# A fused attention-and-GLU backward kernel: fewer all-DVE rows, shorter row groups, paired half matmuls, TensorE transposes at the end of the heads, reordered W_q^T and W_o loads

## The chip, the cores and the metric

The kernel runs on one core of a Trainium2 chip. The time is that of one execution on the device, in microseconds (us); a lower one is better. Comparisons are between medians of several executions. A core has a matrix engine (PE, with its weight loads PEld), a vector engine (DVE), a scalar engine (ACT), a general engine (POOL) and a queue engine (SP) that issues transfers. Each runs its own instructions in order and waits for the others by semaphores.

## The reference

The forward function and its gradient by every weight, by x, and by the key and value caches (S = 2048 rows, D = 576, H = 32 heads of 128, F = 4608):

```python
xn = _layernorm(x)
q = (xn @ wq).reshape(B, Sq, H, Dh).transpose(0, 2, 1, 3)
scores = einsum("bhqd,bhkd->bhqk", q, k_cache) * (Dh ** -0.5)
p = softmax(scores)
s = einsum("bhqk,bhkd->bhqd", p, v_cache).transpose(0, 2, 1, 3).reshape(B, Sq, H * Dh) @ wo
h = sigmoid(xn @ w_gate) * (xn @ w_up)
g = silu(h @ w_down)
out = x + s * g
_out, _vjp = jax.vjp(f, x, k_cache, v_cache, wq, wo, w_gate, w_up, w_down)
return (_out, *_vjp(grad_out))
```

The argument B_x is not used. All arrays are bf16.

## The kernel before

The program is a sequence of stages on one core, each fully unrolled, with the rows in 16 tiles of 128 (NT = 16) and D in four tiles of 128 and a last one of 64 (DL = 4 is its number, KL = 64).

*Stage A* (lines 191 to 349) norms x, makes gate and up products and stores three [2048, 4608] arrays a, b, h. Its last contraction tile has only 64 rows, and gate and up share one weight tile there: `rest` (298 to 303) issues a pair of matmuls, one on partitions 0 to 63 and one on 64 to 127. *Stage A2* (351 to 413) makes h @ w_down, and dS for the projection, kept transposed in `dsT`; the normed x is kept transposed in `xnT`.

*The heads* (416 to 806) take most of the time. A head is laid out in 64 units of its own time scale, HEAD = 64. In the first 32 (the P half) every two units hold one row of P: `s_half` twice (2 matmuls of 512 columns into one of two PSUM buffers of `ps_big`, then a DVE pass with a running minimum), then `s_exp` on ACT. In the second 32 (the dS half) they hold one row of dS: `dp_half` twice. Its second half always goes through DVE in one pass (`scalar_tensor_tensor`, line 592); its first half goes through ACT (line 595) and a DVE product (`ds_mul`, 599), but for the rows in `STT2`, which DVE takes wholly. P and dS of two rows (a pair, 1 MB) are then transposed by one DMA on the SP queue (`trans_dma`, 603), into one of four buffers (`wpt`), and `row_mm` (620) multiplies the result with V or K, four rows (a group) at a time, spread over ROW_W units from unit XR + 8g on. The key and value gradients (`kv_mm`, 641 and 644) are spread over the time that is left by `level`, which fills each unit up to an even load. Transposes on PE and projections for this head and the next one (`prep_...`, `proj`) stand at positions given in tables (QT_AT to QN_AT), and use one PSUM bank, `ps_tr`.

All of it is collected as (position, function) by `at` and `anchor`, sorted, and issued in that order; PE, DVE and ACT keep it (`MAN`), the SP and POOL queues get an order of the compiler's own. At the end of the last head `load_wo` (457) loads W_o over `xnT` and `dsT`, five loads on SP from unit 50 on in program order.

*The projection stage* (808 to 884) multiplies each row tile's transposed attention output (`oT`, loaded by a transposing DMA from `on2_d`, five buffers, line 843) with W_o, makes the output and `doB`, the gradient on the GLU's side, and transposes that into `doBT` (`transpose_doB`). Its fifth tile holds 64 rows of doB in partitions 64 to 127 and zeros below. W_down^T is loaded likewise by `load_wdT` (857), in three thirds, the two others during the next stage. PE, DVE, ACT, SP and POOL keep the program's order here.

*Stage B1* (886 to 981) runs over 18 blocks of 256 columns of F. `make_dh` makes dh for 16 row tiles, five matmuls of 256 columns each (the fifth with the zero half), two row tiles in one PSUM buffer of two, then an ACT copy and two DVE products. `make_dwd` makes the gradient of w_down for 128 rows, twice per block. Then the gradients of w_up and w_gate follow (967, and in column halves 975). `turn` (152) is called throughout: it transposes a stored key or value gradient of one head by DMA and stores the one loaded by the call before; there are 46 of them.

*Stage C2* (985 to 1056) makes the gradients of W_o and W_q, with W_up^T and W_gate^T loaded by the way. *The tail stage* (1058 to 1139) makes dx in eight blocks of 256 rows, each in eight passes (`do_pass`): three with du, three with dg, two with dq, the last two with W_q^T in four groups of eight heads (`load_wqT`). The first two blocks run their first six passes first and then the last two. `finish` ends a block. SP keeps the program's order in B1, C2 and the tail stage.

Of the kernel before, what the change touches and what calls it, by code (L numbers as in the profile page):

```python
# [13 lines left out]
P = 128  # L14
# [81 lines left out]
def kernel(  # L96
# [324 lines left out]
    STT2 = {0, 5, 10}  # L421
    with tc.tile_pool(name="ld2", bufs=2) as ld2, tc.tile_pool(name="ld1q", bufs=1) as ld1q, \
# [192 lines left out]

        def row_mm(bx, hs, T, rhs, qt, kt, sink):
# [81 lines left out]
        XR, ROW_W = 16.8, 6.9  # L698
# [3 lines left out]
        KT_AT, DON_AT, VT_AT, QN_AT = (37.2, 40.0, "s"), (8.6, 22.0, "v"), (0.2, 10.4, "s"), (24.2, 28.2, "s")  # L702
# [51 lines left out]
        WO_AT = 50.0  # L754
        MAN = {mybir.EngineType.PE, mybir.EngineType.DVE, mybir.EngineType.Activation}
        for h in range(H):
# [19 lines left out]
            for qt in range(NT):  # L776
# [32 lines left out]
    if True:  # L809
# [3 lines left out]
        nc.vector.memset(doBT[:P - KL, DL, :], 0.0)  # L813

        def transpose_doB(pool, st_):
# [5 lines left out]
            alt.copy(doBT[P - KL:, DL, cols], pt[P - KL:, DL, :])  # L821

# [6 lines left out]
        with tc.tile_pool(name="c1b", bufs=1, side="right", reuse_waits="tile") as blk, \  # L829
# [60 lines left out]
        with tc.tile_pool(name="b1o", bufs=2, reuse_waits="tile") as outp, tc.tile_pool(name="b1k", bufs=2, reuse_waits="tile") as tkp, tc.tile_pool(name="b1t", bufs=3, reuse_waits="tile") as tmpp, \  # L890
                tc.tile_pool(name="b1r", bufs=2, reuse_waits="tile") as dblk, \
                tc.tile_pool(name="b1l", bufs=1, reuse_waits="tile") as ldp, \
                tc.tile_pool(name="b1ps", bufs=2, space=PSUM, reuse_waits="tile") as ps, \
                tc.tile_pool(name="b1pa", bufs=2, space=PSUM, reuse_waits="tile") as psa, \
# [17 lines left out]
            for fb in range(F // FB):  # L912
# [5 lines left out]
                def make_dh():  # L918
                    for st in range(NT):
                        srows = slice(st * P, (st + 1) * P)  # L920
                        if st % 2 == 0:
                            dh = ps.tile([P, 2, FB], f32, name="dh")
                        for i, (d0, kd) in enumerate(dts):
                            kk = kfull(i, kd)
# [247 lines left out]
```

## Time and profile before

| what | us |
|---|---|
| median of 3 runs | 5063.81 (5054.67 to 5084.64) |
| the profiled execution | 5069.4 |
| its span, first to last instruction | 5067.4 |
| PE busy | 4914.0 (97%) |
| DVE busy | 3098.3 (61%) |
| ACT busy | 2390.4 (47%) |
| POOL busy | 1504.2 (30%) |
| heads without the last one | about 530 to 3530, 98.1 each from the tenth on |
| last head | 3530 to 3660 |
| projection stage | 3660 to 3804 |
| stage B1, 18 blocks | 3804 to 4391, 32.5 each |
| stage C2 | 4391 to 4643 |
| tail stage | 4643 to 5067 |

A line of the list of waits reads: engine, what it was about to do, what ended the wait, then total us, number, longest. In a timeline each row has start, length, engine, line, operation, output and inputs, shape and count, and in brackets the idle time before it and what ended it. "DMA to landing" is from a transfer's issue to its last byte. Busy time of PE counts pipelined matmuls, whose lengths overlap; their spacing is that of their starts.

### The profile page before, as it was taken

The page shows a single profiled execution, that of the slowest core. Times are in us where ns is not written, and L with a number is a line of the kernel's source. Part 1 is how long each engine was busy: PE and PEld are TensorE (multiplying, and loading weights), DVE is VectorE, ACT ScalarE, POOL GpSimd, SP SyncE. Part 2 cuts the span into 40 slices and gives each one's busy share as a digit, 9 for nine tenths or more (in the row PEclk, how much of TensorE's full clock was granted, in tenths as well). Part 3 has the DMA queues.
Part 4 walks back from the last instruction along what each step waited for, and adds up shares of the span by engine and source line. Part 5 has one row for each costly group of instructions (what it writes and reads, how often), then busy time and mean ns, then how long its engine had stood idle before and what let it go on. Part 6 is the DMA issues. An engine that isn't in the chain of part 4 may idle for free.

```text
span 5067.4 us, 107190 instructions
## 1 busy us (share of the span) xinstructions
PE 4914.0 (97%) x45178; PEld 3188.2 (63%) x45968; DVE 3098.3 (61%) x4853; ACT 2390.4 (47%) x3035; POOL 1504.2 (30%) x2197
## 2 busy tenths in 40 slices
PE   9998999999999999999999999999889999999999
PEld 3344777777766666666666666666547778755454
DVE  6555878887887888888788888888533222110101
ACT  5533656665666666566566666656302222100000
POOL 4322333333333333333333333332322323211000
PEclk9999999999999999999999999999999999999999
DMA  7875999999999999999999999999999988899996
GB/s 255 271 219 140 204 201 207 202 209 208 209 205 208 209 201 207 208 203 207 209 209 212 205 208 210 204 202 213 222 182 273 232 225 218 253 267 235 199 211 140
DMA packets 2865204, 1077.14 MB, mean 213 GB/s; under 512 B 2672336, under 2 KB 2795216, under 8 KB 2864720
## 3 DMA queue, kind: packets, MB, share of 16 engines
q1 hardware_dynamic: 2779456, 784.45, 86.6%
q0 software_dynamic: 85264, 285.79, 19.7%
q8 instruction: 359, 5.88, 0.5%
q14 instruction: 125, 1.02, 0.1%
HBM read 172.54 MB, written 225.12 MB: 78 GB/s over the span
## 4 chain that ended last, share of the span: by engine, by line
PE 84%; DVE 5%; issue 4%; DMA 3%; POOL 3%; SPq 0%; ACT 0%; DVEq 0%; POOLq 0%; ACTq 0%
PE acc L620 16%; PE acckv L644 9%; PE acc L1101 7%; PE sp L556 7%; PE dp L589 6%; PE accw L967 5%; PE acckv L641 5%; PE accp L513 4%; PE dh L925 3%; PE acc L392 3%; PE accd L943 3%; PE g_ps L295 2%; PE acc L1025 2%; PE u_ps L295 2%; PE acct L520 2%
## 5 line engine op out<-in xcount | busy, mean ns | idle before, releaser
L568 ACT ACTIVATE Pq<-sneg,nm 128x2048 bf16<-128x2048 bf16 x512 | 1025.9, 2004 | 212.0 <-DVE sneg L558 169.3
L592 DVE SCALAR_TENSOR_TENSOR dSq<-dp,delta,Pq 128x1024 bf16<-128x1024 f32 x608 | 770.8, 1281 | 390.8 <-PE dp L589 384.4
L620 PE MATMUL acc<-Kn,dST 128*128 128x128 bf16 x8192 | 955.2, 219 | 22.5 <-DMA dST<-dSq 6.4
L620 PE MATMUL acc<-Vn,PT 128*128 128x128 bf16 x8192 | 957.9, 219 | 15.9 <-DMA PT<-Pq 6.5
L620 PEld LDWEIGHTS <-dST 128*128 128x128 bf16 x8192 | 670.9, 98 | 363.9 <-DMA dST<-dSq 10.7
L620 PEld LDWEIGHTS <-PT 128*128 128x128 bf16 x8192 | 665.3, 98 | 329.8 <-DMA PT<-Pq 7.6
L558 DVE TENSOR_SCALAR_CACHE_REDUCE sneg<-sp,nm 128x1024 bf16<-128x1024 f32 x512 | 656.7, 1283 | 132.8 <-PE sp L556 101.1
L595 ACT ACTIVATE t<-dp,negdelta 128x1024 bf16<-128x1024 f32 x416 | 463.5, 1114 | 510.3 <-PE dp L589 419.8
L558 DVE TENSOR_SCALAR_CACHE_REDUCE sneg<-sp 128x1024 bf16<-128x1024 f32 x512 | 624.7, 1220 | 92.9 <-PE sp L556 45.7
L589 PE MATMUL dp<-VT,dOT 128*128 128x512 bf16 x1943 | 587.1, 379 | 26.4 <-DVE dSq L592 26.2
L556 PE MATMUL sp<-KT,QT 128*128 128x512 bf16 x1922 | 583.2, 380 | 7.3 <-DVE sneg L558 6.5
L644 PE MATMUL acckv<-Pq,dOn 128*128 128x512 bf16 x1312 | 487.5, 380 | 5.8 <-POOL dOn L576 5.8
L644 PE MATMUL acckv<-dSq,Qn 128*128 128x512 bf16 x1355 | 490.2, 380 | 1.2
L599 DVE TENSOR_TENSOR dSq<-t,Pq 128x1024 bf16<-128x1024 bf16 x416 | 304.5, 732 | 0.0
L576 POOL TENSOR_TENSOR dOn<-dOn,rinv_all 128x256 bf16<-128x256 bf16 x256 | 157.2, 614 | 390.2 <-DVE rinv_all L572 322.7
L967 PEld LDWEIGHTS <-xn_all 128*128 128x128 bf16 x2304 | 224.2, 98 | 27.8
L1117 DVE SCALAR_TENSOR_TENSOR junk<-dxn,xn_all 128x576 f32<-128x576 f32 x16 | 12.1, 758 | 370.9 <-ACT dxn L1112 370.9
L1101 PEld LDWEIGHTS <-cf 128*128 128x128 bf16 x2304 | 145.8, 98 | 145.6 <-DMA cf<-du_d 5.6
L513 PE MATMUL accp<-xnT,wq_h 128*128 128x512 bf16 x609 | 227.8, 384 | 4.4 <-ACT KT L40 1.1
L641 PE MATMUL acckv<-dOn,Pq 128*128 128x128 bf16 x2304 | 217.3, 219 | 2.8 <-POOL dOn L576 1.4
L674 POOL TENSOR_TENSOR prod<-ou,dOn 128x512 f32<-128x512 bf16 x128 | 154.8, 1209 | 207.5 <-ACT ou L40 206.7
L641 PE MATMUL acckv<-Qn,dSq 128*128 128x128 bf16 x2304 | 213.9, 219 | 1.4
(188 smaller groups left out, 7461.6 us busy)
## 6 DMA issues: line engine op xcount, KB each, us to landing
out_dram<-turn SPq DMA_DIRECT2D x46, 512.0 KB, 4.7
h_d<-h_row POOLq DMA_DIRECT2D x48, 384.0 KB, 2.9
a_d<-a_row POOLq DMA_DIRECT2D x48, 384.0 KB, 3.4
b_d<-b_row POOLq DMA_DIRECT2D x48, 384.0 KB, 4.5
a_blk<-a_d SPq DMA_DIRECT2D x18, 1024.0 KB, 6.0
b_blk<-b_d SPq DMA_DIRECT2D x18, 1024.0 KB, 21.7
du_d<-du_blk POOLq DMA_DIRECT2D x18, 1024.0 KB, 8.7
dg_d<-dg_blk POOLq DMA_DIRECT2D x18, 1024.0 KB, 11.7
```

The lines of the kernel that those rows point to most:

```text
L513: nc.tensor.matmul(acc[:], lhsT=w[:, i, :], rhs=(srcT if i < DL else xnT)[:, i, cs], start=(i == 0), stop=(i == DL))
L556: nc.tensor.matmul(sp[:, c * CH:(c + 1) * CH], lhsT=hs.QT[:, qs], rhs=hs.KT[:, hf * HW_ + c * CH: hf * HW_ + (c + 1) * CH], start=True, st ...
L558: nc.vector.tensor_scalar(sneg[:, hf * HW_:(hf + 1) * HW_], sp[:], -SCALE, None if hf == 0 else nm[:, hf - 1:hf], op0=ALU.mult, op1=ALU.mi ...
L568: nc.scalar.activation(Pq, sneg[:], AF.Exp, bias=nm[:, hf:hf + 1], scale=-1.0, accum_out=hs.rs_all[:, qt:qt + 1])
L589: nc.tensor.matmul(dp[:, c * CH:(c + 1) * CH], lhsT=hs.dOT[:, qs], rhs=hs.VT[:, hf * HW_ + c * CH: hf * HW_ + (c + 1) * CH], start=True, s ...
L592: nc.vector.scalar_tensor_tensor(dSq[:, hsl], dp[:], hs.delta[:, qt:qt + 1], Pq[:, hsl], op0=ALU.subtract, op1=ALU.mult)
L595: nc.scalar.activation(t[:], dp[:], AF.Identity, bias=hs.negdelta[:, qt:qt + 1], scale=1.0)
L620: nc.tensor.matmul(bx.acc[:, j, :], lhsT=T[qt][:, kt, :], rhs=getattr(hs, rhs)[:, kt, :], start=(kt == 0), stop=(kt == NT - 1))
L641: nc.tensor.matmul(bx.acc[i][:, j * P:(j + 1) * P], lhsT=slabs[qt][:, k0 + j * P:k0 + (j + 1) * P], rhs=w, start=(qt == 0 and j == 0), sto ...
L644: nc.tensor.matmul(bx.acc[i][:], lhsT=w, rhs=slabs[qt][:, k0:k0 + CH], start=(qt == 0), stop=(qt == NT - 1))
L967: nc.tensor.matmul(acc[:kd, :FB], lhsT=xn_all[:, st, d0:d0 + kd], rhs=blk_[:, st, :], start=(st == 0), stop=(st == NT - 1))
L1101: nc.tensor.matmul(accs[sl][j][:, :nn], lhsT=ch[:, kk, sl * P:(sl + 1) * P], rhs=w_[:, n0:n0 + nn], start=(pi == 0 and kk == 0), stop=(las ...
```

## The change

1. `STT2` goes from rows 0, 5 and 10 to row 0. `ROW_W` goes from 6.9 to 6.7 units, the first position of `DON_AT` from 8.6 to 8.9, and the last quad of the first kv group comes no earlier than 8.1 units after its base instead of 7.4.
2. `load_wo` issues from ACT instead of SP, in 15 pieces of two or three heads, one every 4 units from unit 1.3 of the last head on.
3. In the last head the P pair of rows 14 and 15 and the dS pairs of rows 6 and 7 and of rows 14 and 15 are transposed by PE (`pe_pair`) and copied from PSUM, and not by DMA.
4. `doBT`'s fifth tile gets the 64 rows in both partition halves, and so does the last tile of W_down^T, by a POOL transfer from partitions 64 to 127 to 0 to 63 that waits for the transposing one. `make_dh` is made in halves of eight row tiles, with four PSUM buffers: the first four matmuls of all eight tiles, then the eight fifth ones in pairs, one on each half of the partitions, of row tiles two apart. In all blocks but the first the order is now dh half, dwd half, dh half, dwd half. dwd has one PSUM pair in place of two.
5. Stage C2 has one `turn` less and the tail stage's turns stand in passes 1, 3 and 5 of blocks 2 to 6. W_q^T groups 2 and 3 are loaded two passes later in the second block. The last passes of the first two blocks alternate: pass 6 of both, then pass 7 of both.

```diff
-    STT2 = {0, 5, 10}
+    STT2 = {0}
-            nc.sync.dma_start(dst, A_wo[h0 * P:h1 * P, :].rearrange("(h p) d -> p h d", p=P))
+            nc.scalar.dma_start(dst, A_wo[h0 * P:h1 * P, :].rearrange("(h p) d -> p h d", p=P))
...
+        def pe_pair(T, pairs, qt, name, n, pool, tag, i, eng):
+            if i == 0:
+                t_ = wpt.tile([P, 2 * NT, P], bf, name=name, tag="PT")
+                for j in range(2):
+                    T[qt + j] = t_[:, j * NT:(j + 1) * NT, :]
+            pt = pool.tile([P, n, P], bf, name="ptr", tag=tag)
+            for m in range(n):
+                j, kt = divmod(i * n + m, NT)
+                nc.tensor.transpose(pt[:, m, :], pairs[qt][:, j, kt * P:(kt + 1) * P], ident[:])
+            j, kt = divmod(i * n, NT)
+            alt.copy(T[qt + j][:, kt:kt + n, :], pt[:], eng=eng)
...
-        XR, ROW_W = 16.8, 6.9
+        XR, ROW_W = 16.8, 6.7
-        KT_AT, DON_AT, VT_AT, QN_AT = (37.2, 40.0, "s"), (8.6, 22.0, "v"), (0.2, 10.4, "s"), (24.2, 28.2, "s")
+        KT_AT, DON_AT, VT_AT, QN_AT = (37.2, 40.0, "s"), (8.9, 22.0, "v"), (0.2, 10.4, "s"), (24.2, 28.2, "s")
-                    pos = max(pos, 4.0 * (n // 4) + 7.4, DON_AT[1] + 2.0 if n >= NT else 0.0)
+                    pos = max(pos, 4.0 * (n // 4) + (8.1 if n // 4 == NT // 2 - 1 else 7.4), DON_AT[1] + 2.0 if n >= NT else 0.0)
-        WO_AT = 50.0
+        WO_AT = [(i, min(i + 2, 14)) for i in range(0, 14, 2)] + [(14, WX)] + [(i, min(i + 2, WX + WD)) for i in range(WX, WX + WD, 2)]
+        P_PE = {NT - 2: (35.5, 37.5, 39.5, 41.5)}
+        DS_PE = {6: (48.5, 50.5, 52.5, 54.5), NT - 2: (65.5, 67.0)}
...
-                    at(p1 + PT_AT, trans_P, hs, qt - 1)
-                    at(p2 + DST_AT, trans_dS, hs, qt - 1)
+                    if h == H - 1 and qt - 1 in P_PE:
+                        for i, p_ in enumerate(P_PE[qt - 1]):
+                            at(b + p_, pe_pair, hs.PT, hs.Pp, qt - 1, "PT", 8, ps_tr, "tr", i, "s")
+                    else:
+                        at(p1 + PT_AT, trans_P, hs, qt - 1)
+                    if h == H - 1 and qt - 1 in DS_PE:
+                        for i, p_ in enumerate(DS_PE[qt - 1]):
+                            if len(DS_PE[qt - 1]) == 4:
+                                at(b + p_, pe_pair, hs.dST, hs.dSp, qt - 1, "dST", 8, ps_tr, "tr", i, "s")
+                            else:
+                                at(b + p_, pe_pair, hs.dST, hs.dSp, qt - 1, "dST", NT, ps_big, "big", i, "sv"[i])
+                    else:
+                        at(p2 + DST_AT, trans_dS, hs, qt - 1)
...
-        for k, (h0, h1) in enumerate(((0, 8), (8, 16), (16, WX), (WX, WX + 7), (WX + 7, WX + WD))):
-            if h0 < H - 1:
-                at(bl + WO_AT + 3 * k, load_wo, h0, min(h1, H - 1))
+        for k, (h0, h1) in enumerate(WO_AT):
+            at(bl + 1.3 + 4 * k, load_wo, h0, h1)
...
-        nc.vector.memset(doBT[:P - KL, DL, :], 0.0)
...
             alt.copy(doBT[P - KL:, DL, cols], pt[P - KL:, DL, :])
+            alt.copy(doBT[:KL, DL, cols], pt[P - KL:, DL, :])
...
                 nc.sync.dma_start_transpose(wdT_h[k][:, i, :], B_w_down[k * FH:(k + 1) * FH, dlo[i]:dlo[i] + P])
+                if i == DL:
+                    nc.gpsimd.dma_start(wdT_h[k][:KL, DL, :], wdT_h[k][P - KL:, DL, :])
...
-                tc.tile_pool(name="b1ps", bufs=2, space=PSUM, reuse_waits="tile") as ps, \
-                tc.tile_pool(name="b1pa", bufs=2, space=PSUM, reuse_waits="tile") as psa, \
+                tc.tile_pool(name="b1ps", bufs=4, space=PSUM, reuse_waits="tile") as ps, \
+                tc.tile_pool(name="b1pa", bufs=1, space=PSUM, reuse_waits="tile") as psa, \
...
+                def make_dh(half):
+                    w_ = wdT_h[fb * FB // FH]
+                    sts = range(half * NT // 2, (half + 1) * NT // 2)
+                    dhs = [ps.tile([P, 2, FB], f32, name="dh") for _ in sts[::2]]
+                    for k, st in enumerate(sts):
+                        for i in range(DL):
+                            nc.tensor.matmul(dhs[k // 2][:, k % 2, :], lhsT=doBT[:, i, st * P:(st + 1) * P], rhs=w_[:, i, fh],
+                                             start=(i == 0 and k % 2 == 0), stop=False)
+                    for k in (0, 1, 4, 5):
+                        for j in range(2):
+                            rs = slice(j * KL, (j + 1) * KL)
+                            st = sts[k + 2 * j]
+                            nc.tensor.matmul(dhs[k // 2 + j][:, k % 2, :], lhsT=doBT[rs, DL, st * P:(st + 1) * P], rhs=w_[rs, DL, fh],
+                                             start=False, stop=(k % 2 == 1))
+                    for k, dh in enumerate(dhs):
...
                 else:
-                    make_dh()
                     for fl in range(FB // P):
+                        make_dh(fl)
                         make_dwd(fl)
...
-                if hg < NHG - 1:
+                if hg < NHG - 2:
                     turn(tkp)
...
+            WQ_AT = [(0, 3), (0, 5), (1, 3), (1, 5)]
...
-                if sbi == 0 and pi in (3, 5):
-                    load_wqT((3, 5).index(pi))
-                elif sbi == 1 and pi in (1, 3):
-                    load_wqT(2 + (1, 3).index(pi))
-                elif sbi and sbi < NSB - 1 and (pi % 4 == 1 or (pi == 3 and sbi > 1)):
+                if (sbi, pi) in WQ_AT:
+                    load_wqT(WQ_AT.index((sbi, pi)))
+                elif 1 < sbi < NSB - 1 and pi in (1, 3, 5):
                     turn(tkp)
...
-            order_ = [(sbi, pi) for sbi in range(2) for pi in range(NPF)] + [(sbi, pi) for sbi in range(2) for pi in range(NPF, len(passes))]
+            order_ = [(sbi, pi) for sbi in range(2) for pi in range(NPF)] + [(sbi, pi) for pi in range(NPF, len(passes)) for sbi in range(2)]
```

More of the change, by code (lines that the diff above doesn't have):

```diff
@@ L1 @@
+import itertools
 from contextlib import ExitStack
@@ L917 @@
                 dg_blk = dblk.tile([P, NT, FB], bf, name="dg_blk")
[L918 to L924, printed above, removed]
-                            nc.tensor.matmul(dh[:, st % 2, :], lhsT=doBT[:kk, i, srows], rhs=wdT_h[fb * FB // FH][:kk, i, fh], start=(i == 0), stop=(i == DT - 1))
-                        if st % 2 == 1:
-                            s2 = slice(st - 1, st + 1)
-                            dhc = tmpp.tile([P, 2, FB], bf, name="dhc")
-                            nc.scalar.copy(dhc[:], dh[:])
-                            nc.vector.tensor_tensor(du_blk[:, s2, :], dhc[:], a_blk[:, s2, :], op=ALU.mult)
-                            nc.vector.tensor_tensor(dg_blk[:, s2, :], dhc[:], b_blk[:, s2, :], op=ALU.mult)
-                    nc.gpsimd.dma_start(du_d[:, fcols].rearrange("(t p) f -> p t f", p=P), du_blk[:])
-                    nc.gpsimd.dma_start(dg_d[:, fcols].rearrange("(t p) f -> p t f", p=P), dg_blk[:])
@@ L1079 @@
             accs_ = {}
+            ncq = itertools.count()
+            WQ_AT = [(0, 3), (0, 5), (1, 3), (1, 5)]
             def do_pass(sbi, pi):
```

13 lines of the change are left out of this document (11 added, 2 removed).

## The prediction

> **What bounds the kernel now.** First the page's head, then busy time by stage, to see which engine is full where.
>
> ```profile
> span 5067.4 us, 107190 instructions
> 530.00:3530.00 3000.00, 2933.32 (x29506) 2011.22 (x30058) 2424.89 (x3520) 1921.14 (x2153) 1022.14 (x1425) 1.00 1.17 207
> 3530.00:3660.00 130.00, 108.22 (x944) 69.20 (x961) 78.58 (x113) 57.16 (x64) 35.17 (x48) 0.93 1.14 219
> 3660.00:3804.00 144.00, 130.46 (x1073) 69.24 (x1093) 48.38 (x75) 7.69 (x31) 33.78 (x63) 0.96 1.16 191
> ```
>
> Columns: stretch, its length, busy time of PE, PE's weight loads, DVE, ACT and POOL, clock, DMA share, GB/s. PE is full in the heads (first row: all but the last head), and short by 22 us in the last head (second row) and by 14 us in the projection after it (third). So a gain comes either from fewer PE slots or from PE's stops. The list of PE's waits, over heads 0 to 30, the last head, the projection stage and the tail stage:
>
> ```profile
> PE dp L589 <- DVE dSq L592: 25.1, 30, 0.8
> PE acckv L644 <- POOL dOn L576: 5.1, 22, 1.4
> ...
> PE acc L872 <- DMA oT<-on_d: 7.4, 1, 7.4
> PE acc L620 <- DMA PT<-Pq: 6.1, 3, 4.5
> PE acc L620 <- DMA dST<-dSq: 3.6, 2, 2.9
> ...
> PE acc L872 <- DMA oT<-on_d: 12.3, 2, 9.8
> ...
> PE acc L1101 <- DMA cf<-du_d: 4.9, 2, 3.1
> PE acc L1101 <- DMA cf<-dg_d: 2.0, 1, 2.0
> ```
>
> One dp stop of 0.84 us falls in each head. The timeline of DVE and PE shows where:
>
> ```profile
> 2032.79 2.47 DVE L592 SCALAR_TENSOR_TENSOR dSq<-dp,delta,Pq 128x1024 bf16<-128x1024 f32 x2
> 2034.12 0.59 PE L589 MATMUL dp<-VT,dOT 128*128 128x512 bf16 x2 [0.85 <-DVE dSq L592]
> ```
>
> That is row 10, whose two halves both go to DVE, just behind a delta reduction, a kv copy and a product (three at 0.68). PE needs the first half's PSUM buffer and gets it 0.85 late. Rows 0 and 5 stop nobody.
>
> Next to PE runs the SP queue, the instructions of the transposing line:
>
> ```profile
> L603 SPq DMA_TRANSPOSE PT<-Pq  x256: 4778/5628/8863, 484.3 to 3590.6; - x128
> L603 SPq DMA_TRANSPOSE dST<-dSq x256: 4716/5892/9762, 530.8 to 3643.5; - x128
> ```
>
> Added up in the timeline these 16 per head hold SP 5.98 us each, with 0.1 between: 97.3 us of a head's 98.1. They start on average 3 to 4 us after their slab is complete, and land 4 us (median) before the first weight load that reads them. SP is thus nearly a second bound.
>
> **Row 0 alone on DVE; shorter row groups.** Row 10's first half becomes an ACT pass (1.11, mean of L595) plus a DVE product (0.68) in place of 1.28 of DVE. ACT stands idle for the 2.06 us up to 2031.55, and the copies of wo's transpose (0.86 for two) move behind the new pass. The buffer is free at about 2032.2 where PE wants it at 2033.3, so the stop goes: 25.1. Row 5 the same, for nothing. ACT gains 2.2 us per head at 64% busy (1921/3000). The last quad of the first kv group, put at 8.1 rather than 7.4, waits out POOL's scaling: 5.1 + 1.2 (the like wait of L641). Together 31 us, or 1.0 a head, for a pace of 97.1.
>
> But SP needs 97.3. Going through the 480-odd pairs with their own durations, against a PE that has these stops no longer, the pairs come late by 13 to 16 us in sum; with each transpose 1% shorter by 2, with 1% longer by 32. Row groups of 6.7 instead of 6.9 units free a buffer 0.3 us earlier and ask for a second pair 0.15 us earlier: nothing either way against 4 us. I take **-15**, bounds -31 and 0.
>
> **Last head.** Three pairs (P rows 14-15, dS rows 6-7 and 14-15) leave SP: 3 x 6 = 18 us of it. PE makes 96 transposes instead; eight of L520 take 0.49 us on their weight loads, so 12 x 0.49 = 5.9 us, and ACT eight-block copies of 0.99 each, with ACT at 44% (57/130) in that stretch, and one larger DVE copy. No projection for a next head uses that PSUM bank any more. Removed: the dST stops (3.6) and the stop on the first oT (7.4), as SP reaches oT earlier. The PT stops (6.1) came while 4.5 MB of W_o were issued between transposes from SP; the same bytes now go in 15 pieces from ACT over the whole head, so half the bytes remain beside the P transposes: 4 of the 6.1 go. After its two long stops PE ran at half speed for 5.5 and 4.6 us (512-column matmuls at 0.63 instead of 0.38): 5.0 lost, 4 regained. Fifteen issues of 0.58 (SP's row for these loads) hold ACT 9 us, which it has. Sum: -3.6 - 7.4 - 4 - 4 + 5.9 = **-13**; bounds -20 (all stops and clock go) and +6 (only the transposes are felt).
>
> The Trainium skill (DMA: Bandwidth & Descriptors, Issuing engines are not separate DMA queues) says that another issuing engine saves only issue time, since all share the same 16 DMA engines. By it only SP's 3.3 us of W_o issues (three of 0.58, 0.58 and 0.95) would come back of the PT stops, near the 4 taken.
>
> **Projection stage.** From its ninth tile on, each oT load is issued just as its buffer is freed (five buffers, unchanged), and 8 to 15 us per transpose beside the 144 KB loads and stores makes the 12.3 us late. An earlier start of the queue does not change that part: 0, bounds -14 and +8. New: POOL waits for the last W_down^T transpose before it copies its 64 rows, with the row loads for tiles 14 and 15 behind it. That transpose landed at 3796.5, when PE ended tile 14 (3795.6); loads land 4 us later: DVE's last products and two doB transposes may slip, **+1** (0 to 3). The two later copies stand before an h block that is needed over one block (32 us) later. Sixteen small doBT copies and one memset lie on DVE and ACT, idle there: 0.
>
> **dh pairs.** Of 40 slots per half block, 8 fifth matmuls become 4 pairs with 64 rows each. Stage A's timeline has such pairs:
>
> ```profile
> 149.70 0.81 PE L295 MATMUL u_ps<-wu_sb,xnT 128*128 128x512 bf16 x3
> 150.44 0.39 PE L303 MATMUL g_ps<-wl_sb,xnT 64*128 64x512 bf16 x1
> 150.44 0.39 PE L303 MATMUL u_ps<-wl_sb,xnT 64*128 64x512 bf16 x1
> 150.67 0.38 PE L303 MATMUL g_ps<-wl_sb,xnT 64*128 64x512 bf16 x1
> ...
> 150.98 1.04 PE L295 MATMUL g_ps<-wg_sb,xnT 128*128 128x512 bf16 x4
> ```
>
> and the chain of waits has a whole dh block (start, length):
>
> ```profile
> 3838.32 8.84 PE dh L925 x80
> ```
>
> The two start together, so a pair costs one slot; but going in costs 0.09 more than the 0.22 spacing (150.44 instead of 150.35), coming out again 0.09. A dh slot is (8.84 - 0.27) / 79 = 0.108. Per half: 4 x 0.108 saved less 0.18, 0.25; two weight loads per slot may cost another 0.01 each. 36 halves: **-8**, bounds -15.6 (no cost of switching) and +6.5 (pairs run one by one, 36 x 0.18). One accumulator pair instead of two is hidden: half a dh (4.1 us) lies between the halves of dwd, and its copies take 0.69. The last product of a half ends about 3.5 us after its dh, under a dwd half of 3.9.
>
> The Trainium skill (TensorEngine Tiling (Array Packing), Key Properties) says that changing the tiling mode drains the engine. A full drain, as an estimate 0.27 - 0.11 = 0.16 per switch, would leave 0.11 per half, 4 us in all; stage A's 0.09 is shorter, and the sum goes by it.
>
> **Tail.** One turn fewer ahead of the first cf load, W_q^T groups 2 and 3 two passes later, pass 6 of both column blocks before pass 7: the late cf loads get 6.6 us of transposes (five at 1.3) less ahead of them. The cq loads (5 us each, PE 7.7 a pass) follow just in time. **-5** of 6.9; bounds -7 and 0. The last turn is now loaded in the sixth block's sixth pass and stored by the call behind the loop, after the last dx store on SP: a turn store takes 3.2 us to land, the dx store 1.8, so **+2**.
>
> **Sum.** -15 - 13 + 0 + 1 - 8 - 5 + 2 = -38. The profiled execution's 5069.4 (span 5067.4 and 2.0 around) would be 5031; the median of the runs shown, 5063.8, is 5.6 lower, so **5026**.
>
> **Rivals.**
> *All stops go*: SP keeps up (its durations shrink with PE's stops), -31; last head -20; dh -10; tail -5. -66, 4998. For it: 52 places in heads 2 to 30 where SP stood idle, 46 us in sum. Against: nine heads in a row (14 to 22) without any.
> *SP takes the stop over*: heads give nothing, the last head -5, dh -8, tail -3: -16, 5048. For it: those nine heads averaged 98.4 us.
> *Pairs don't pair*: 256-column pairs need two weight loads in 0.108 us. dh +6.5 instead of -8: 5040. Against: L975, two column halves of the same width, one pair per 0.11.
> *ACT held by its loads* (slower): if each W_o issue holds ACT until the transpose before it has landed (9.2 us, median landing), eight of them in the P half cost 74, less some 6 us of slack there: 68 - 38 = +30, 5094. It decides from 5.5 us per issue on (44 - 6 = 38). Against: SP's own W_o issues took 0.58 to 0.95 directly behind transposes. None of the rows shows an issue from ACT during transposes.
>
> **How the numbers follow.** Forecast 0.60 (its own range 5012 to 5040), all stops go 0.16, SP takes over 0.15, no pairs 0.03, ACT held 0.06. A change under 0.5% (25 us: 5038.5) can't be told from none. Faster: 0.56 of the forecast's 0.60, all of 0.16, 0.02 of the third: 0.74. Slower: the last, 0.06. Same: 0.20. Range 4996 to 5052: from the first rival through the second.
>
> **What would show it.** dp's waits on DVE fall from 30 to about none, and waits on PT and dST rise from 3 to some 15 us over the heads: right; if they rise by 30, the second rival. dh blocks of 2 x 4.1 us with K=64 matmuls starting in twos: right; one by one, the third. No 7.4 us stop at the first oT. ACT's W_o issues under 1 us each. A turn store landing last. It is wrong if head pace stays at 98.1, or if a new stop appears in each head.

## The result and the profile after

| | before | after |
|---|---|---|
| median, us | 5066.76 (17 runs, 5048.19 to 5084.64) | 5039.6 (17 runs, 5021.89 to 5055.04) |
| ratio, 95% interval | | 0.995 (0.9935 to 0.9965) |
| profiled execution, its span | 5069.4, 5067.4 | 5044.53, 5042.7 |

The changed kernel is 27 us faster. The forecast was 38 (5026), its range 4996 to 5052. A table by stage shows how the parts of the sum came out. Its limits are starts of single instructions in the two profiled executions: first exp of head 0, first exp of head 31, last row matmul of the last head, last matmul with W_o, last of B1, last of C2, last matmul of PE, end.

| stage | before | after | difference | forecast |
|---|---|---|---|---|
| up to head 0's first exp | 479.7 | 486.4 | +6.7 | 0 |
| 31 heads | 3048.7 | 3042.8 | -5.9 | -15 |
| last head | 128.6 | 117.8 | -10.8 | -13 |
| projection stage | 146.7 | 135.3 | -11.4 | +1 |
| B1 | 587.3 | 581.4 | -5.9 | -8 |
| C2 | 251.8 | 253.8 | +2.0 | 0 |
| tail and end | 424.7 | 425.3 | +0.6 | -3 |
| span | 5067.4 | 5042.7 | -24.7 | -38 |

The first row's code is unchanged. All later profiles of this study have 478 to 483 there; this execution was long by chance.

The page's head, and the stages' busy times (stretch, length, busy PE, PE's weight loads, DVE, ACT, POOL, granted clock, DMA share, GB/s):

```profile
span 5042.7 us, 108373 instructions
PE 4952.7 (98%) x46064; PEld 3173.9 (63%) x46064; DVE 3049.5 (60%) x4861; ACT 2466.5 (49%) x3116; POOL 1532.1 (30%) x2200
```
```profile
530.00:3530.00 3000.00, 2967.92 (x30135) 2017.22 (x30133) 2393.28 (x3525) 1992.14 (x2221) 1052.24 (x1431) 1.00 1.18 207
3530.00:3648.00 118.00, 109.95 (x1057) 72.18 (x1056) 78.81 (x115) 69.41 (x75) 34.18 (x45) 0.99 1.16 217
3648.00:3783.00 135.00, 132.07 (x1109) 69.76 (x1107) 45.95 (x81) 13.33 (x38) 36.22 (x66) 1.00 1.15 198
```

In the last head PE was idle 22 us of 130 and is now idle 8 of 118; in the projection stage it was 14 of 144 and is 3 of 135. PE's waits over heads 0 to 30, the last head, the projection stage and the tail stage:

```profile
PE acc L633 <- DMA dST<-dSq: 16.6, 13, 2.8
PE acc L633 <- DVE dq_n L704: 12.3, 30, 0.4
PE dp L590 <- DVE dSq L593: 1.1, 2, 0.8
PE acc L633 <- DMA PT<-Pq: 0.8, 3, 0.3
PE acckv L657 <- POOL dOn L577: 0.3, 1, 0.3
...
PE acc L899 <- DMA oT<-on_d: 3.5, 1, 3.5
PE acc L633 <- DMA PT<-Pq: 2.3, 3, 1.1
...
PE acc L899 <- DMA oT<-on_d: 2.9, 3, 1.8
...
PE acc L1137 <- DMA cf<-du_d: 2.8, 1, 2.8
PE acc L1137 <- DMA cq<-dq_d: 2.6, 2, 2.3
```

The dp stop is gone (25.1 to 1.1), the stops on dOn too (6.5 to 0.3). Against this stand 12.3 us of new stops on `dq_n`, 0.41 in each head, which nothing in the forecast's sum names, and waits on dST that rose from 2.8 to 16.6. The timeline (start, length) shows the new stop:

```profile
2558.01 0.59 PE L557 MATMUL sp<-KT,QT 128*128 128x512 bf16 x2
2558.44 0.38 PE L657 MATMUL acckv<-dSq,Qn 128*128 128x512 bf16 x1
2559.23 0.22 PE L633 MATMUL acc<-Kn,dST 128*128 128x128 bf16 x1 [0.41 <-DVE dq_n L704]
2559.29 0.61 PE L521 MATMUL acct<-ident,dOT 128*128 128x128 bf16 x8
...
2557.28 1.28 DVE L559 TENSOR_SCALAR_CACHE_REDUCE sneg<-sp,nm 128x1024 bf16<-128x1024 f32 x1 [0.41 <-PE sp L557]
2558.49 0.69 DVE L704 TENSOR_TENSOR dq_n<-acc,rsc 128x512 bf16<-128x512 f32 x1
```

PE begins the fourth dS row group (unit 8.8 of the next head) and needs the PSUM buffer that DVE is still emptying for the third. The eight transposes of dOT, moved from 8.6 to 8.9, now come right behind that matmul; at 8.6 they lay in front of it.

Some late dST pairs make long stops. Behind the two longest (2.67 in head 7, 2.80 in head 23) stands a stretch at half clock. Head 23, POOL's timeline, then the stretches:

```profile
2813.62 0.60 POOL L481 DMA_DIRECT2D Vn<-in_A_v_cache_dram  x1 [4.21 <-PE acc L633]
2816.84 0.83 POOL L695 DMA_DIRECT2D on_d<-o_n  x1 [0.29 <-POOL o_n L694]
2820.66 0.54 POOL L494 DMA_DIRECT2D wo_h<-in_A_wo_dram  x1 [2.99 <-PE acct L502]
```
```profile
2819.00:2824.00 5.00, 5.00 (x54) 3.43 (x52) 4.59 (x6) 3.55 (x5) 1.72 (x4) 1.00 1.51 141
2824.00:2829.00 5.00, 2.24 (x15) 0.96 (x12) 2.48 (x3) 1.11 (x1) 0.98 (x2) 1.00 0.94 174
2829.00:2834.00 5.00, 4.96 (x31) 2.91 (x32) 1.88 (x2) 1.27 (x2) 0.00 (x0) 0.66 1.25 238
```

In the same 10 us as a V load, a row store and a W_o load, one transpose held SP for 9.9 us instead of 6 and landed 15.6 us after its issue, at 2829.0. PE stands for 2.8 us in the second row, and in the third its clock is 0.66.

### The profile page after: what moved, and what is told of

It reads as the page before. It is cut to its first block, busy times and chain, and to the rows that moved or that the text cites. A ratio compares the mean times of both kernels' runs of the same rounds, so it can differ in the third digit from the quotient of the medians.

```text
span 5042.7 us, 108373 instructions
## 1 busy us (share of the span) xinstructions
PE 4952.7 (98%) x46064; PEld 3173.9 (63%) x46064; DVE 3049.5 (60%) x4861; ACT 2466.5 (49%) x3116; POOL 1532.1 (30%) x2200
## 4 chain that ended last, share of the span: by engine, by line
PE 86%; DMA 7%; issue 3%; DVE 2%; POOL 1%; SPq 0%; ACT 0%; DVEq 0%; POOLq 0%; ACTq 0%
PE acc L633 16%; PE acckv L657 11%; PE sp L557 8%; PE acc L1137 8%; PE dp L590 7%; PE acckv L654 5%; PE accw L1002 5%; PE accp L514 5%; DMA dST<-dSq 3%; PE acc L393 3%; PE accd L977 3%; PE dh L951 2%; PE acc L1060 2%; PE acct L521 2%; PE acc L899 2%
## 5 line engine op out<-in xcount | busy, mean ns | idle before, releaser
L633 PE MATMUL acc<-Kn,dST 128*128 128x128 bf16 x8192 | 946.2, 219 | 30.8 <-DMA dST<-dSq 16.6
L593 DVE SCALAR_TENSOR_TENSOR dSq<-dp,delta,Pq 128x1024 bf16<-128x1024 f32 x544 | 694.7, 1282 | 394.3 <-PE dp L590 389.4
L633 PE MATMUL acc<-Vn,PT 128*128 128x128 bf16 x8192 | 920.3, 219 | 3.4 <-DMA PT<-Pq 3.1
L633 PEld LDWEIGHTS <-PT 128*128 128x128 bf16 x8192 | 653.8, 98 | 333.9 <-DMA PT<-Pq 6.1
L596 ACT ACTIVATE t<-dp,negdelta 128x1024 bf16<-128x1024 f32 x480 | 535.1, 1115 | 460.0 <-PE dp L590 455.8
L557 PE MATMUL sp<-KT,QT 128*128 128x512 bf16 x2048 | 610.8, 380 | 6.6 <-DVE sneg L559 6.5
L590 PE MATMUL dp<-VT,dOT 128*128 128x512 bf16 x2048 | 609.9, 379 | 2.1 <-DVE dSq L593 1.1
L657 PE MATMUL acckv<-dSq,Qn 128*128 128x512 bf16 x1472 | 537.5, 380 | 0.0
L657 PE MATMUL acckv<-Pq,dOn 128*128 128x512 bf16 x1472 | 528.8, 379 | 0.3 <-POOL dOn L577 0.3
L600 DVE TENSOR_TENSOR dSq<-t,Pq 128x1024 bf16<-128x1024 bf16 x480 | 343.0, 714 | 0.0
L1153 DVE SCALAR_TENSOR_TENSOR junk<-dxn,xn_all 128x576 f32<-128x576 f32 x16 | 12.1, 758 | 370.7 <-ACT dxn L1148 370.7
L1148 ACT ACTIVATE dxn<-acc 128x512 f32<-128x512 f32 (+1 forms) x32 | 12.9, 407 | 403.0 <-issue 301.6
```

The lines of the kernel that those rows point to most:

```text
L557: nc.tensor.matmul(sp[:, c * CH:(c + 1) * CH], lhsT=hs.QT[:, qs], rhs=hs.KT[:, hf * HW_ + c * CH: hf * HW_ + (c + 1) * CH], start=True, st ...
L590: nc.tensor.matmul(dp[:, c * CH:(c + 1) * CH], lhsT=hs.dOT[:, qs], rhs=hs.VT[:, hf * HW_ + c * CH: hf * HW_ + (c + 1) * CH], start=True, s ...
L593: nc.vector.scalar_tensor_tensor(dSq[:, hsl], dp[:], hs.delta[:, qt:qt + 1], Pq[:, hsl], op0=ALU.subtract, op1=ALU.mult)
L596: nc.scalar.activation(t[:], dp[:], AF.Identity, bias=hs.negdelta[:, qt:qt + 1], scale=1.0)
L633: nc.tensor.matmul(bx.acc[:, j, :], lhsT=T[qt][:, kt, :], rhs=getattr(hs, rhs)[:, kt, :], start=(kt == 0), stop=(kt == NT - 1))
L657: nc.tensor.matmul(bx.acc[i][:], lhsT=w, rhs=slabs[qt][:, k0:k0 + CH], start=(qt == 0), stop=(qt == NT - 1))
```

## The experiments

Each kernel is the changed one with the edit shown. The stage times below are from one profiled execution each, with the limits of the table above. As executions of one kernel differ by up to 48 us here, the stage that an edit touches tells more than the total.

| run | 31 heads | last head + projection | B1 | C2 | tail + end | median | ratio to before |
|---|---|---|---|---|---|---|---|
| before | 3048.7 | 275.3 | 587.3 | 251.8 | 424.7 | | |
| after | 3042.8 | 253.1 | 581.4 | 253.8 | 425.3 | 5039.6 | 0.995 (0.9935 to 0.9965) |
| e1_don | 3065.1 | 263.5 | 579.3 | 252.6 | 422.2 | 5030.4 | 0.9939 (0.9906 to 0.9972) |
| e2_skip | 3030.7 | 245.0 | 580.6 | 252.1 | 424.6 | 5015.9 | 0.9902 (0.9865 to 0.9939) |
| e3_heads | 3059.2 | 250.9 | 579.5 | 254.2 | 423.1 | 5047.0 | 0.9968 (0.9947 to 0.9989) |
| e4_lastdma | 3042.4 | 284.4 | 579.7 | 254.6 | 425.1 | 5057.9 | 0.9982 (0.9964 to 1.0) |
| e5_wosp | 3048.1 | 258.7 | 579.3 | 253.0 | 421.9 | 5037.2 | 0.9963 (0.9946 to 0.9979) |
| e6_nopair | 3051.8 | 252.4 | 586.8 | 252.0 | 421.6 | 5047.0 | 0.9984 (0.9967 to 1.0) |
| e7_tail | 3048.2 | 250.6 | 579.3 | 252.0 | 425.8 | 5040.4 | 0.9968 (0.9956 to 0.9979) |
| e8_xr178 | 3171.8 | 251.5 | 579.3 | 252.9 | 423.3 | 5171.4 | 1.0224 (1.0199 to 1.0248) |
| e9_xr188 | 3057.7 | 262.6 | 579.3 | 252.5 | 424.6 | 5062.5 | 1.0012 (0.9997 to 1.0027) |
| e10_nokv | 3018.4 | 258.2 | 579.3 | 252.8 | 422.0 | 5010.7 | 0.9909 (0.9884 to 0.9935) |
| e11_layout | 3029.8 | 247.8 | 579.3 | 291.4 | 425.3 | 5035.0 | 0.9949 (0.993 to 0.9968) |
| e12_best | 3012.4 | 255.3 | 580.9 | 251.8 | 423.2 | 5008.8 | 0.9898 (0.9875 to 0.9921) |

**The new stop.**

```diff
-        KT_AT, DON_AT, VT_AT, QN_AT = (37.2, 40.0, "s"), (8.9, 22.0, "v"), (0.2, 10.4, "s"), (24.2, 28.2, "s")
+        KT_AT, DON_AT, VT_AT, QN_AT = (37.2, 40.0, "s"), (8.6, 22.0, "v"), (0.2, 10.4, "s"), (24.2, 28.2, "s")
```

> Changed kernel with dOn's first transposes back at unit 8.6, ahead of the start of dS row group 3 at 8.8. Theory A (the new stop on dq_n exists because those eight transposes, 0.49 us, no longer lie between two row groups): the 30 stops of 0.41 go, 12 us, and the stretch from the first exp of head 0 to that of head 31 falls from 3042.8 to about 3031; the whole by 12. Theory B (the SP queue's transposes, near their bound, give any PE gain back as waits on dST and PT): the dq_n stops go, but waits on dST rise by 6 to 12 us from 16.6 and the stretch stays between 3036 and 3043. Theory C (the dq_n stop comes from DVE's fuller order, not from the place of the transposes): the stops stay at 0.4 each.

PE's waits in the heads of this run:

```profile
PE acc L633 <- DMA dST<-dSq: 32.7, 27, 4.3
PE acct L521 <- ACT dOT L41: 7.3, 30, 0.2
PE acc L633 <- DMA PT<-Pq: 3.2, 4, 1.1
```

No stop on `dq_n` is left: theory A names the right cause. The transposes at 8.6 now wait 0.24 for ACT's copy of dOT, so a head without a late pair takes 97.08 instead of 97.25, a gain of 0.17 and not 0.41. Theory B holds too in this profile: dST waits doubled, and it was among the longest of the seven executions (5063; the median is 5030). By the totals the two kernels can't be told apart, as the intervals overlap.

**One transpose less per head.**

```diff
         def trans_dS(hs, qt):
+            if hs.h < H - 1 and qt == NT - 2:
+                hs.dST[qt:qt + 2] = hs.dST[qt - 2:qt]
+                return
```

> Changed kernel with one transfer less on the SP queue in heads 0 to 30: the dS pair of rows 14 and 15 isn't transposed, its row matmuls read the pair before (so dq's last rows of these heads are not the reference's). PE, DVE and ACT do as much as before. Theory B (the queue is what holds the heads above their own floor): 15 x 6 = 90 us of SP's 97 per head, waits on dST (16.6 us) and half-clock stretches go, and the stretch of 31 heads falls from 3042.8 to 9 x 98.2 + 22 x 97.3 = 3024, some 19 us. Rival (the loss over the floor is PE's, DVE's or ACT's): within 5 us of 3042.8.

```profile
PE acc L636 <- DVE dq_n L707: 12.8, 31, 0.4
PE acc L636 <- DMA dST<-dSq: 9.6, 4, 7.1
```

The stretch, 3030.7, lies 12 under the lowest of five profiles with all transposes (3042.4 to 3051.8, see below), and the median of the whole is 24 lower. Twenty-one of the 31 heads take their floor (98.18 up to the ninth, 97.25 from the eleventh on) to within 0.02, against 18 in the changed kernel. What is left of dST waits is mostly one stop of 7.1, in head 1. So what holds the changed heads above their floor is the transposing, and not PE's, DVE's or ACT's own order.

**The same queue, less traffic beside it.**

```diff
-            hs.Kn = ld2.tile([P, NT, P], bf, name="Kn")
...
+            if h == 0:
+                hs.Kn = ld2.tile([P, NT, P], bf, name="Kn")
...
+            hs.Kn, hs.Vn = kv0
```

> Changed kernel with K and V loaded for head 0 alone, whose tiles all heads use (so what follows from K and V is not the reference's); 1 MB less per head of the other queue's 3.5 MB; SP still makes 16 transposes per head. Theory G (all queues share the engines that move the data, which the transposes fill): a transpose takes SP some 4% less in the mean (6.0 to 5.75), dST waits fall below 8, stretch of heads 3024 to 3034. Rival (SP's queue is slow by itself): mean 5.95 to 6.05, stretch 3042 to 3052.

```profile
PE acc L638 <- DVE dq_n L709: 12.7, 31, 0.4
PE acc L638 <- DMA PT<-Pq: 2.0, 1, 2.0
PE dp L595 <- DVE dSq L598: 1.6, 2, 0.8
```

Not one wait on dST is listed, with all 16 transposes made. The times that they held SP, in heads 0 to 30, added up from the trace:

| run | transposes | mean us | over 9 us | longest |
|---|---|---|---|---|
| before | 495 | 5.96 | 3 | 9.8 |
| after | 495 | 5.98 | 10 | 10.5 |
| e1_don | 495 | 6.06 | 11 | 13.7 |
| e2_skip | 465 | 5.78 | 4 | 12.3 |
| e10_nokv | 495 | 5.67 | 0 | 7.9 |
| e12_best | 496 | 5.84 | 5 | 11.4 |

Theory G holds, and the gain is more than it said (3018.4 against 3024 to 3034): 1 MB less in the other queue shortens the mean transpose by 5%, and those over 9 us vanish. At 5.98 and 0.1 between, 16 need 97.3 us, which is the floor itself; at 5.67 they need 92.3, and 25 of the 31 heads take their floor. The Trainium skill (DMA: Bandwidth & Descriptors, Issuing engines are not separate DMA queues) says that transfers from any issuing engine run on the same 16 DMA engines and interleave; the 5.98 against 5.67 agrees.

**Later row groups.**

```diff
-        XR, ROW_W = 16.8, 6.7
+        XR, ROW_W = 17.8, 6.7
...
-                rows(b + H1 + 8 * g + XR, hs, hs.dST, "Kn", g, dq_sink(hs, g))
+                rows(b + H1 + 8 * g + XR - (h == H - 1) * 0.33 * g, hs, hs.dST, "Kn", g, dq_sink(hs, g))
```

> Changed kernel with each row group one unit (1.52 us) later (XR 17.8; in the last head the four dS groups close up to end where they did). In the changed kernel's trace a pair's buffer is free 2 us before its data is there, so SP loses nothing, and every pair has 1.5 us more between landing and first read. Also group 3 of dS now starts at 9.8, behind dOn's transposes at 8.9. Theory B (late pairs are those whose slow transposes exceed a margin of 3 to 4 us): waits on dST fall from 12 to 33 us over the heads to under 8, the dq_n stops (12.3) go to under 3, and the stretch of 31 heads falls to 3012 to 3030, 15 to 30 under the changed kernel. Theory F (the queue is so near its bound that any margin is used up): dST waits stay above 10, the stretch 3035 or more.

The second kernel has 18.8, 0.66 and dOn's first position at 9.9.

> As the one before, two units later (XR 18.8), with dOn's first transposes at 9.9 to stay between the two dS row groups. Theory B: margin 3 us more, nearly all dST waits gone (under 4), stretch 3008 to 3022. Theory F (buffers now free 1 us after the data): SP starts later, dST or PT waits above 10, stretch not below that of the one before.

Neither became faster, for a reason that no theory had: the shift brings new stops on ACT and DVE. Waits of the first, then of the second:

```profile
PE dp L590 <- DVE dSq L593: 60.4, 30, 2.1
PE acc L633 <- ACT ou L41: 60.3, 86, 1.0
PE acc L633 <- DMA dST<-dSq: 9.7, 11, 2.2
PE acc L633 <- DVE dq_n L704: 5.7, 29, 0.2
```
```profile
PE acct L521 <- DVE dOn L43: 30.5, 30, 1.0
PE acc L633 <- DMA dST<-dSq: 11.4, 11, 3.5
```

In the first, 120 us are such stops. Half of them stand behind a DVE product that falls beside POOL's scaling of Qn: 30 of these took 3.08 us instead of 0.68, and each of the 30 dp stops ends 2.44 after one. In the second, dOn's transposes at 9.9 and V's at 10.4 want the same PSUM bank, 1.0 per head. On the question itself, two units (3 us) of margin left dST waits at 11.4, which for the second is theory F's sign; SP went from transpose to transpose with 0.1 between ahead of each late pair, as a backlog has it. The first shows something else. Its heads take about 102 us, some 5 more than SP needs, and SP had gaps of 1.0 to 2.3 us shortly before ten of its eleven late pairs. Yet each of these held SP for 10.0 to 12.6 us and landed 15.3 to 20.0 after its issue. So a pair can be late without a backlog, by being slow itself; margin alone did not remove either kind.

**The heads' part undone.**

```diff
-    STT2 = {0}
+    STT2 = {0, 5, 10}
-        XR, ROW_W = 16.8, 6.7
+        XR, ROW_W = 16.8, 6.9
...
```

(with `DON_AT` at 8.6 and 7.4 for the last quad)

> Changed kernel with the heads' part undone: rows 0, 5 and 10 on DVE, row groups of 6.9 units, dOn at 8.6, last quad at 7.4. Theory B (SP gives most of it back; the 5.9 us between the two profiles are real): stretch of 31 heads 3046 to 3052, whole time 4 to 9 above the changed kernel. Rival (the stops that went are worth their 31 less 12 for the new stop, and the changed kernel's profile was an unlucky one with its two half-clock stretches): 3058 to 3065, some 19 above.

The median is 7.4 above the changed kernel's, within theory B's 4 to 9, though the two intervals overlap. The profiled stretch (3059.2) would have spoken for the rival, but it holds 12.1 us of dST waits against 2.8 in the profile of before, with the same code in the heads. The stretch scatters by that much: five profiles with the changed heads (after, e4 to e7) have 3042.4 to 3051.8, mean 3046.7; two with the old ones 3048.7 and 3059.2. So the heads' part gains something between 2 and 12 us, and less than the 19 of the rival.

**Last head: which part made the gain.**

```diff
-        P_PE = {NT - 2: (35.5, 37.5, 39.5, 41.5)}
-        DS_PE = {6: (48.5, 50.5, 52.5, 54.5), NT - 2: (65.5, 67.0)}
+        P_PE = {}
+        DS_PE = {}
```

> Changed kernel with the last head's three pairs transposed by DMA on SP again; W_o stays on ACT. Theory D (the pairs that left SP let oT and W_down^T start earlier): last head and projection stage, 117.8 + 135.3 together, get back 15 us or more of the 22 they gained: 268 or more. Theory E (W_o's pieces on ACT are what freed SP): they get back less than 6: under 259. As PE has 96 transposes less (5.9 us by the estimate), a small gain, down to 250, would also be E.

```diff
-            nc.scalar.dma_start(dst, A_wo[h0 * P:h1 * P, :].rearrange("(h p) d -> p h d", p=P))
+            nc.sync.dma_start(dst, A_wo[h0 * P:h1 * P, :].rearrange("(h p) d -> p h d", p=P))
...
-            at(bl + 1.3 + 4 * k, load_wo, h0, h1)
+            at(bl + 50.0 + 3 * k, load_wo, h0, h1)
```

(five pieces instead of 15)

> Changed kernel with W_o's loads as before: five on SP from unit 50 of the last head on. Theory D (the three pairs on PE made the gain of the last head and the projection stage): last head and projection stage together stay within 6 us of 253.1. Theory E (W_o's move made it): 15 us or more come back, 268 or more.

With the pairs on SP, the two stages take 284.4, 31 more than the changed kernel and 9 more than before the change, as these waits of its last head show:

```profile
PE acc L633 <- DMA dST<-dSq: 14.9, 8, 5.8
PE acc L899 <- DMA oT<-on_d: 6.5, 1, 6.5
PE acc L633 <- DMA PT<-Pq: 5.2, 3, 3.7
```

With W_o back on SP they take 258.7, 5.6 more, inside the 245 to 263.5 of the profiles whose last head is unchanged. So it is theory D: the three pairs on PE made the gain, and W_o's move made none that shows. A gain or loss of some 6 us by that move could not be seen in one profile of such scatter.

**dh without pairs.**

```diff
-                    for k in (0, 1, 4, 5):
-                        for j in range(2):
...
+                    for k, st in enumerate(sts):
+                        nc.tensor.matmul(dhs[k // 2][:, k % 2, :], lhsT=doBT[:, DL, st * P:(st + 1) * P], rhs=w_[:, DL, fh],
+                                         start=False, stop=(k % 2 == 1))
```

> Changed kernel with dh's fifth matmuls unpaired: eight of 128 rows (half of them zeros) per half in place of eight of 64; halves, order and buffers stay. If pairing is worth what the forecast took, 4 x 0.108 less 0.18 per half, a dh half goes from 4.14 to about 4.39 and stage B1 gets 9 us longer (590). If the halved order and not the pairs made B1's 5.9 us, within 2 us of 581.4. If pairs cost more than they save, shorter than 579.

The end of one dh half, in the changed kernel and in this one:

```profile
3925.75 0.82 PE L951 MATMUL dh<-wdT,doBT 128*128 128x256 bf16 x6
3926.50 0.61 PE L957 MATMUL dh<-wdT,doBT 64*128 64x256 bf16 x8
3927.05 4.09 PE L977 MATMUL accd<-doB,h_blk 128*128 128x512 bf16 x32
```
```profile
3925.79 0.82 PE L951 MATMUL dh<-wdT,doBT 128*128 128x256 bf16 x6
3926.44 1.04 PE L954 MATMUL dh<-wdT,doBT 128*128 128x256 bf16 x8
3927.31 4.08 PE L974 MATMUL accd<-doB,h_blk 128*128 128x512 bf16 x31
```

From the start of the last full-height run to the next stage's first matmul: 1.30 with pairs, 1.52 without, 0.22 for each of 36 halves, 7.9 in all. The stage says 7.5 (586.8 against 579.3, which seven other profiles have to within 0.1; four have 579.5 to 580.9, and the changed kernel's own 581.4 holds 2.1 us of short stops at its start). The halved order alone is worth 0.5 (587.3 to 586.8, one profile each).

**The tail.** Stage C2's turns, the tail's turns, W_q^T loads and pass order as before:

```diff
-                if hg < NHG - 2:
+                if hg < NHG - 1:
...
-            order_ = [(sbi, pi) for sbi in range(2) for pi in range(NPF)] + [(sbi, pi) for pi in range(NPF, len(passes)) for sbi in range(2)]
+            order_ = [(sbi, pi) for sbi in range(2) for pi in range(NPF)] + [(sbi, pi) for sbi in range(2) for pi in range(NPF, len(passes))]
```

> Changed kernel with stage C2's turns, the tail stage's turns, W_q^T loads and pass order as before. Forecast's step (5 us less of waits on cf, 2 more at the end): tail and end together 3 us longer, 428. By the two profiles (waits only moved from cf to cq): within 2 us of 425.3, C2 as after, 252 to 254.

Tail and end took 425.8, within 2 of the changed kernel's 425.3, as the second expectation had it and not the forecast's. Nine other profiles with the changed tail have 421.6 to 425.1. The part is worth 0 to 4 us; one profile can't say more.

**Row results by head.** The rows' share of traffic is as large as K and V's. In the changed kernel a store of o or dq writes runs of 256 bytes.

```diff
-    on2_d = dram.tile([S, HD], bf, name="on2_d")
+    on2_d = dram.tile([H, P, NT, P], bf, name="on2_d")
...
-                nc.gpsimd.dma_start(on2_d[g * CH:(g + 1) * CH, hs.h * P:(hs.h + 1) * P].rearrange("(t p) d -> p t d", p=P), o_n[:])
+                nc.gpsimd.dma_start(on2_d[hs.h][:, gs, :], o_n[:])
...
-                    nc.sync.dma_start_transpose(oTs[st_][:], on2_d[st_ * P:(st_ + 1) * P, :])
+                    nc.sync.dma_start_transpose(oTs[st_][:], on2_d[:].rearrange("h p t d -> (h p) t d")[:, st_, :])
...
+                elif (sbi, pi) == (NSB - 1, 1):
+                    turn(tkp, False)
```

(dq likewise; cq is held by row tile; dOn at 8.75)

> Changed kernel with the row results (o and dq, 1 MB per head) kept in DRAM as [head, partition, tile, 128] instead of [row, head x 128], so that a store writes 1 KB runs instead of 256 bytes: a quarter of the packets for the same bytes. oT and cq are then transposed from rows of 256 bytes (cq in two transposes of half the size). Also dOn's first transposes at 8.75 and the last turn's store in the second pass of the last block. Theory G2 (other transfers slow the transposes by their packets, the row stores most: alongside them a transpose of the changed kernel took 6.28 us, without 5.38): mean transpose 5.7 or less instead of 5.98, dST waits under 5, and with the dq_n stop gone a stretch of 31 heads of 3008 to 3020, whole time 5000 to 5015. Rival (it goes by bytes): mean 5.9 to 6.05, dST waits 15 or more, stretch 3030 to 3055. Projection stage 130 to 140 and tail 413 to 419 if transposes from 256-byte rows take as long as before; longer by 10 or more if not. End 7 instead of 8.4.

The mean transpose took 5.95, dST waits were 14.9 and the stretch 3029.8: in this profile the price does not go by the length of a run, which is the rival. (The next kernel, with the same heads, has a mean of 5.84, between the two theories.) Transposes from 256-byte rows took SP no longer: in the tail two of 2.49 us in the mean stand for one of 5.19, and the projection stage took 131.8 here and 144.1 in the next kernel, where ten profiles with the old rows have 131.6 to 143.1. The end fell to 7.1. What went wrong is C2, 37.6 us longer, with 25.9 us of waits on its loads of `onb`. There one load per block had become four, which read runs of 4 KB in DRAM and write runs of 256 bytes in SBUF. The next kernel mends that (the diff is against this one; dq likewise, and the blocks lie by head in SBUF):

```diff
-                    for hl in range(HG):
-                        nc.sync.dma_start(held[hg][0][:, :, hl * P:(hl + 1) * P], on2_d[hg * HG + hl])
+                    nc.sync.dma_start(held[hg][0][:], on2_d[hg * HG:(hg + 1) * HG].rearrange("h p t d -> p h t d"))
```

> The kernel before this one (layout by head, dOn at 8.75, last turn's store earlier) with stage C2's blocks held as [128, 4 heads, 16, 128] and loaded by one transfer each with 4 KB runs on both sides, where it had four with runs of 256 bytes in SBUF. If those short runs made stage C2 37.6 us longer, C2 falls from 291.4 to 250 to 258, and the whole from 5035 to 4993 to 5003 in the median, 1.2% under the kernel before the change. If the loads of 4 KB runs from DRAM are slow whatever the other side, C2 stays above 280. The heads as there: stretch 3005 to 3030, no dq_n and no dOT stops.

C2 is back at 251.8. What the DMA queues moved in stage C2, in the kernel with the short runs and in this one:

```profile
DMA packets 204492, 67.02 MB, mean 230 GB/s; under 512 B 200506, under 2 KB 200506, under 8 KB 204474
DMA packets 88418, 66.92 MB, mean 266 GB/s; under 512 B 76768, under 2 KB 76768, under 8 KB 88400
```

For the same bytes the first has 123,700 more packets under 512 bytes, as many as 60 loads of 512 KB in pieces of 256 bytes make. So the short runs are the likely cost. That four transfers became one again changed with them, and no run parts the two.

The median is 5008.8, 5.8 above the expected band, and its interval (0.9875 to 0.9921) lies under the changed kernel's: this version beats both, by 1.0% the kernel before and by some 30 us the changed one. Its waits in the heads:

```profile
PE acc L633 <- DMA dST<-dSq: 4.2, 5, 1.7
PE acckv L654 <- POOL dOn L577: 1.2, 1, 1.2
PE acc L633 <- DMA PT<-Pq: 0.9, 1, 0.9
```

Neither `dq_n` nor dOT stops PE with dOn at 8.75. Some 12 us are the removed `dq_n` stops and 1.3 the earlier store. The rest, some 17, is fewer late pairs (mean 5.84), and why is open: e11 has the same heads and had 14.9 of dST waits in a profiled execution that was long for it (5054.6, median 5035.0), and no run had the layout alone.

## Why the prediction was right or wrong

The time (5039.6) lies in the range and 13.6 above the forecast.

- **Stops in the heads: -31** was right for what goes (25.1 to 1.1 and 6.5 to 0.3). The claim that the changed positions bring nothing new failed: the forecast booked the later positions only against POOL's scaling of dOn, and did not ask what those eight transposes had covered on PE. 12.3 us came back as `dq_n` stops; e1 shows the cause. It is the "new stop in each head" that the text named as a sign of error.
- **SP hands back to -15**: right in kind. dST and PT waits rose from 3.2 to 17.4, close to the "some 15" named, and e2 and e10 show by two ways that the transposes hold the heads above PE's own pace. Not foreseen was that a late pair of 2 us and more can also cost clock. The term is worth 7.4 by e3's median and 5.9 by the two profiles instead of 15, both within the scatter of 2 to 12: mis-sized mainly by the new stop.
- **Last head: -13** against -10.8: sized well, though its split was not. The 4 us booked for W_o's move are not seen in e5, and the pairs gave more: with them back on SP (e4) the last head alone took 137.9, 20 more. ACT's 15 issues took 0.37 to 0.44 us each, so *ACT held by its loads* was wrong.
- **Projection stage: 0** was the step that failed most: -11.4. "An earlier start of the queue does not change that part" took the 12.3 us of oT waits for a matter of buffers from the ninth tile on. With three pairs less in the queue the waits fell to 2.9. With the pairs back (e4) they were 9.7 and the stage took 146.5 again, where the ten profiles with the pairs on PE and the old rows have 131.6 to 143.1. How the earlier start works on the later loads is only in part seen. oT's first transpose went out 9.7 us earlier (3628.7 instead of 3638.4), but PE came to the stage 10.1 earlier too, so that lead did not grow. What grew is the lead of the loads behind it: before and in e4 a dS pair still stands behind the first oT load, and the fifth goes out 10.6 and 10.1 us after the stage's start, in the changed kernel 5.5. Why that is enough for the ninth and later ones stays open; the same code left no oT waits in e7 and 2.9 here. The bound of -14 had room for it. POOL's wait for the W_down^T copy cost nothing that is seen.
- **dh pairs: -8** against 7.5 by e6, with the switch at 0.09 a way as read from stage A. The Trainium skill (TensorEngine Tiling (Array Packing), Key Properties) has a drain at each switch and gives no price; the prediction's estimate of a full drain, 0.16 a way, would have left 4 us. The 0.22 saved per half, out of 4 x 0.108, leaves 0.11 a way. *Pairs don't pair* was wrong: the two of a pair start 3 to 4 ns apart.
- **Tail: -5 and +2.** The cf waits fell from 6.9 to 2.8, but cq, "just in time", took 2.6 of it; the later turn store cost 0.9, not 2. The sum, -3 in the forecast, came out as +0.6 in the two profiles, and as 0 to 4 gained by e7.

So 27 were right for a reason half other than the one given: the heads gave 9 less, the projection stage 12 more. That these two nearly cancel is luck. By its own terms the first rival (*all stops go*) lacked a queue that keeps up; the second (*SP takes the stop over*, 5048) came nearer in number than the forecast, but had the last head at -5 and no gain behind it.

## What to carry to other kernels

When a piece of work is moved by a fraction of a unit, ask also what it covered where it stood, not only what it waits for. When an engine's stop is removed beside a queue that is as full as the engine, cut the queue's load at the same time: here 5% shorter transposes brought 24 us in the heads (e10), where removing 30 us of stops had brought 6. Taking a few transfers off a queue ahead of a stage can pay in that stage as well, as the projection stage did here; by which of its loads was not settled.

## What the runs showed of the hardware

- A stop of PE may cost its clock. In thirteen kernels' profiles (all but e8_xr178), from 620 to 3500 us, half clock for 3.4 or 6.8 us set in within 6 us of the start of every stop of 3.0 us or longer (ten), of eleven of the twenty between 1.89 and 3.0, and of none of the thirteen from 1.5 to 1.88. In e8_xr178 it followed seven of 28 stops of 2.05 to 2.23. Half clock over 3.4 us costs, as an estimate, half of that, 1.7; head 23 of the changed kernel took 101.77 instead of 97.25, of which its stop is 2.80. The Trainium skill (TensorE: Matmul & The Clock Gate, What's actually happening) has an idle window of about 3.4 us that runs freely; a stop of 1.94 was enough here, shorter than that.
- In e8_xr178 all 30 DVE products that began 0.61 us before POOL's scaling of Qn (1.91 us) took 3.08 us; the 383 with nothing on POOL beside them took 0.67 to 0.68. Over all 480 the mean was 0.89, in the changed kernel 0.71. That they disturb each other is read from their times alone.
- Loads whose runs are 4 KB in DRAM and 256 bytes in SBUF, four of 512 KB for one of 2 MB, made stage C2 37.6 us longer than in the changed kernel (runs of 1 KB on both sides) and 39.6 longer than with 4 KB on both sides. The packets under 512 bytes were 200,506 instead of 76,768.
